# Threshold attention and a squared-ReLU layer on one core: the order of the first loads, of attention's last two periods, of the second layer's weight loads, and of some sums of x

## The chip, the cores and the metric

The kernel runs on one core of a Trainium2 chip. The metric is the device time of one execution in microseconds (us). TensorE (PE in the profile) does the matrix products, VectorE (DVE), ScalarE (ACT) and GpSimd (POOL) the elementwise work, and SyncE (SP) issues nearly all transfers, in program order.

## The reference

Attention first, on 8 batches, 8 heads, 576 positions and 64 columns, then a layer on 4608 tokens, all in float32 (the two weight matrices come as float64 and are converted in the kernel):

```python
scores = scale * np.matmul(q, k.transpose(0, 1, 3, 2))
thresh = np.max(scores, axis=-1, keepdims=True) - tau
scores = np.where(scores >= thresh, scores, -1000000000.0)
scores = scores - np.max(scores, axis=-1, keepdims=True)
attn = np.exp(scores)
attn = attn / (np.sum(attn, axis=-1, keepdims=True) + 1e-09)
x = np.matmul(attn, v)      # then (B,H,S,D) -> (B*S, H*D) = 4608 x 512
h = np.maximum(x @ w_in, 0.0)        # w_in 512 x 2048
out = h * h @ w_out                  # w_out 2048 x 512
```

## The kernel before, in words

**Attention.** Heads are taken two at a time: 32 pairs, loaded with `load_q`, `load_k` and `load_v`. A pair has four full tiles of 128 queries, and two pairs share a fifth made of their rests, so there are 144 units (`NU`). A period p works on units 2p and 2p + 1 at different stages at once. `period(p)` holds its steps by name, and a list of names gives their order: `CONVERTING` while weight chunks are being converted, `PLAIN` afterwards, and `BEGIN_WITH[p]` for a period with an order of its own (0 and 1 before the change). A trailing "-" means the step of the period before, "--" of two before; `step` first runs any earlier period's step of that name that was not run yet, and each (step, period) runs once.

The steps that matter here: SA, SB and RA, RB are the scores (L458); top is the reduction on VectorE (L476); pow and mask are exp on ScalarE (L486) and masking on VectorE (L491). The masked weights of two units m are turned on TensorE in three fills (`fill`, L402): V covers the first eight of 18 half tiles (chunks 0 to 3), W the two of chunk 4, U the eight of chunks 5 to 8. V and U go to the one buffer pair `pt`, W to two middle banks of the scores' memory `sc`. Q adds the scales (L541). eV, eW and eU copy a fill out to the arena (`filled`, L549, on ScalarE), PV is the product with the values (`values`, L558, 72 matmuls over nine chunks), x copies the result out of banks 0 and 5 of `sc` (L689 on ScalarE, L691 on VectorE), xm scales the rest (L701 on GpSimd) and queues the store to `xT` in DRAM. The program declares by hand which instructions on `sc` do not depend on each other: `touch` records each with its banks and key, and pairs of kinds listed in `MEET` keep their dependency.

**SyncE's order.** The loads of queries and keys are queued in `wanted` and issued a few at a time by the steps "ahead" and "more" (`ahead(5)`); "fetch" issues the load of a weight chunk (L194) two periods ahead; the main loop issues `load_v(p)` after periods 0, 1 and 2 (L337). A pair's keys come with L320 and L327, the queries' rest with L328, into the same tile `rn` as the rest keys. Every transfer waits for the transfer eight places ahead of it in that order to be done, so at most eight are out at once.

**The layers.** Both products are done with seven instead of eight block products, nested twice, so a pass has 7 x 7 = 49 products. `hidden_layer` runs nine passes (`PASSES`): one for the first 512 tokens, six in pairs that share weights, two single ones. After each product a tick runs `also`, in which work for later passes is placed by block i (0 to 6, in the order `OUTER`) and place `at` in it (0 to 6). In `inner` the copy of the first product (L794, ScalarE) and the additions to products (L125, VectorE) free TensorE's six banks; GpSimd adds the finished blocks (L125). `square` squares a finished block (L951, L952) and stores it to `g` in DRAM (L955, or L958 for paired passes), at least six ticks after it is done.

`before_x` makes sums of x for the next pair of passes during passes 0, 2, 4 and 6. A sum (`sum_v`) is a ScalarE copy of one operand to the small buffer `c` (L838) and, a tick later, the operation on VectorE (L122 or L125). The two sums `turned_` read a part of x that is loaded (L820) at block 2, place 1, and are placed at block 3, places 0 and 3.

`output_layer` runs nine times, on the operands g (`load_g`, L1064) and the second layer's weights. These 49 weight tiles stand in DRAM (`w`) and overwrite the first layer's in `wall` once those are done with: `reload(at)` (L1207). Tile `at` is first used at product `at` of the first output pass, that is tick 49 + `at` counted from the start of the last hidden pass. Before the change one reload follows each tick from tick 10 on: 39 in the last hidden pass, ten in the first output pass. In the first output pass `load_g(1, ...)` loads eight tiles at block 2, place 0 (tick 63), and eight at block 2, place 6 (tick 69); the first sums of the second eight are at block 4.

Of the kernel before, what the change touches and what calls it, by code (L numbers as in the profile page):

```python
# [48 lines left out]
def kernel(  # L49
# [322 lines left out]
    behind = mybir.DependencyInfo(mybir.DependencyClass.Sync, mybir.DependencyReason.DATA)  # L372

    Q_RING, K_RING, W_RING = 3, 4, 2
    MEET = (("scores", "turnedq", (Q_RING,)), ("scores", "turnedk", (K_RING,)), ("last scores", "turnedk", (K_RING,)), ("values", "weights", (W_RING,)), ("x", "weights", (W_RING,)))

    def touch(what, made, at, size, key=0):

# [162 lines left out]
                    made = nc.tensor.matmul(to, wide, ident[rows, rows], start=True, stop=True)  # L541
                    touch("turns", made, at + r * BANK, BANK)

    def filled(m, f, pt, at=None):

        first, count = FILLS[f]
        count += 2 * (f == "W")
        to = wT[m][:, ds(weight_at(first) * P, count * P)]
        touch("weights", nc.scalar.copy(joined(to), whole(pt, 0, count)), at, 2 * BANK, m)  # L549

    def values(m):

        for c in range(CH):
            for u in range(2):
                for s, (i, _, count, row) in enumerate(halves(2 * m + u)):
                    for j in range(2):
                        rows = ds(j * D, D)
                        made = nc.tensor.matmul(  # L558
                            sc[ds(u * D, D), ds(5 * j * BANK + row, count)], loaded_v[i][rows, (c - (u != j)) % CH, :],
                            wT[m][rows, ds(weight_at(2 * c + u) * P + row, count)],  # L560
                            start=(c == 0 and s == 0), stop=(c == CH - 1), skip_group_check=True,
                        )
                        touch("values", made, 5 * j * BANK, BANK, m)

    def valued(m):

# [71 lines left out]
        """.split(),  # L638
    }

    def spots():
        return [(sc[:, ds(b * BANK + REST, (FULL + 1) * HALF)], b * BANK) for b in (1, 4)]

    def middle():
        return sc[:, 2 * BANK : 4 * BANK].rearrange("p (r n) -> p r n", r=2)

    def period(p):

# [2 lines left out]
        late, pt = {"W": []}, {}  # L651

        def fills(f, m):
            if has(2 * m):
                pt[f] = pt_pool.tile([P, 2, BANK], FP32, tag="pt", name="pt")
                fill(m, f, pt[f])

        def evict(f, m):
            if has(2 * m):
                filled(m, f, pt[f], 2 * BANK if f == "W" else None)  # L660

        def W():
            if has(2 * m + 2):
                pt["W"] = middle()
                fill(m + 1, "W", pt["W"], 2 * BANK)

        def Q():
            if has(2 * m + 2):
                spread_sums(m + 1, pt["W"], 2 * BANK)

        def turn_some():
            free = None
# [42 lines left out]
        def every(key):  # L715
# [10 lines left out]
            "c1": lambda: convert1(begun(p)), "c2": lambda: convert2(begun(p)),  # L726
            "c3": lambda: convert3(begun(p)), "c4": lambda: convert4(begun(p - 1)),
            "c5": lambda: convert5(begun(p - 1)), "c6": lambda: convert6(begun(p - 1)),
            "s1": lambda: sums_due(p) and sums_step(), "s2": lambda: sums_due(p) and p < 60 and sums_step(), "ahead": lambda: ahead(5), "more": lambda: ahead(5),
            "fetch": lambda: (fetch(begun(p + 2)), fetch(begun(p + 3)) if p > 1 else None), "put": put, "give": lambda: ask(False),  # L730
        }
        steps["over"] = lambda: do(a, "over")
# [170 lines left out]
    def before_x(steps, i, at):  # L903

        if (i, at) in BEFORE_X:
            ask_x(steps, *BEFORE_X[i, at])
        turned_ = lambda: outer_x(steps, minus, 6, 2, None)
        added = lambda: outer_x(steps, plus, 6, 6, 1)
        fourth = lambda: outer_x(steps, minus, 4, 2, 6)
        if i == 4 and at < len(steps):  # L910
            nc.scalar.copy(slot_x(steps[at], 7), slot_x(steps[at], 6))
        work = {
            (3, 0): lambda: turned_()[0:1], (3, 3): lambda: turned_()[1:],
            (4, 2): lambda: added()[0:1], (4, 5): lambda: added()[1:],
            (5, 1): lambda: fourth()[0:1], (5, 4): lambda: fourth()[1:],
            (5, 6): lambda: inner_x(steps, 1),
        }
        return work.get((i, at), list)()
# [242 lines left out]
    with tc.manual_schedule():  # L1161
        with ExitStack() as stack:
# [24 lines left out]
            turn(0, 1, spots(), nc.vector.tensor_copy)()  # L1187
            for p in range(FIRST_PERIOD, NU // 2 + 6):
                run_period(p)
                if 0 <= p < 3:  # L1190
                    load_v(p)
                if X_FIRST <= p < X_FIRST + 4:
                    load_x(0, XPARTS[p - X_FIRST :][:1])
                if p == X_FIRST + 4:
                    summing.append(prepare_x(0, lambda op, out, x, y: op(nc.gpsimd, out, x, y)))
# [6 lines left out]
        def reload(at):  # L1202

            m, k = OUTER[at // 7], INNER[at % 7]
            t = weight_tile(W_OUT, m, k)
            at = 8 * made_at(m) + made_at(k)
            nc.sync.dma_start(out=t[:, :], in_=w_dram[ds(at * P, P), :])  # L1207

        chain_at, over_at = 26 * BANK, 26 * BANK + 2 * BANK
        halves_ = [(m, k, h) for m, k in blocks_out[EARLY:] for h in range(2)]  # L1210
# [69 lines left out]
        for n, (steps, h) in enumerate(PASSES):  # L1280
# [14 lines left out]
            def also(m, at):  # L1295
# [91 lines left out]
```

## Time and profile before

| | us |
|---|---|
| median of 3 runs | 1282.17 (1278.94 to 1284.23) |
| profiled execution | 1281.21 |
| its span, first to last instruction | 1279.1 |
| TensorE busy in the span | 1252.5 |
| attention ends (first product of the hidden layer) | 495.87 |
| first output pass goes on after its first four products | 889.50 |

A timeline row reads: start, duration, engine, line, operation, written <- read, shape, count, and in brackets the idle time of the engine just ahead of it with what ended it. A row of windows reads: the stretch, its length, the busy time of PE, PEld, DVE, ACT and POOL with the number of instructions, the clock granted to TensorE (1.00 is full), the busy share of the transfer engines, and GB/s.

### The profile page before, as it was taken

What the parts mean: (1) busy time and instruction counts of PE and PEld (TensorE: products, weight loads), DVE (VectorE), ACT (ScalarE), POOL (GpSimd) and SP (SyncE); (2) the same over time, 40 slices, a digit from 0 to 9 for tenths busy, and PEclk for the clock granted to TensorE, in tenths of its full rate; (3) what the DMA queues carried; (4) which work ended last, traced back from release to release, by engine and by line L of the source; (5) the groups of instructions that cost most, each with busy time, mean ns of one, the idle gap of its engine ahead of it and who ended that gap; (6) DMA issues with size and microseconds to landing.
All of it is one profiled execution on the core that took longest, in us unless ns stands there. A gap on an engine that the chain in (4) does not pass through costs nothing.

```text
span 1279.1 us, 55422 instructions
## 1 busy us (share of the span) xinstructions
PE 1252.5 (98%) x22991; PEld 1093.8 (86%) x22991; DVE 987.5 (77%) x2384; ACT 845.6 (66%) x1537; POOL 982.4 (77%) x1070
## 2 busy tenths in 40 slices
PE   7999999999999999999999999999999999999998
PEld 5777777777777778988888888999999999999998
DVE  6999999999999995886887877876646654665563
ACT  6999999999999994665765857665424432433240
POOL 2899898877776542987897989858777877787776
PEclk9999999999999999999999999999999999999999
DMA  7566667434333323658767868589654235523511
GB/s 185 131 170 149 176 191 195 117 93 104 85 86 86 80 58 84 203 170 232 209 190 215 229 169 239 164 304 361 240 164 162 65 109 167 167 57 112 167 35 35
DMA packets 291450, 196.81 MB, mean 154 GB/s; under 512 B 100096, under 2 KB 252160, under 8 KB 291200
## 3 DMA queue, kind: packets, MB, share of 16 engines
q1 hardware_dynamic: 289888, 192.87, 52.6%
q8 instruction: 181, 2.97, 1.0%
q14 instruction: 69, 0.57, 0.2%
q10 hardware_dynamic: 1312, 0.41, 0.1%
HBM read 120.85 MB, written 72.35 MB: 151 GB/s over the span
## 4 chain that ended last, share of the span: by engine, by line
PE 74%; DMA 2%; DVE 2%; ACT 1%; issue 1%; SPq 0%; POOL 0%; DVEq 0%; POOLq 0%; ACTq 0%
PE po L799 27%; PE ph L982 18%; PE ph L799 10%; PE sc L558 7%; PE sc L458 6%; PE pt L402 4%; PE sc L541 1%; PE sc L422 1%; DVE arena L125 1%; DMA arena<-g 1%; ACT c L838 1%; PE sc L402 0%; DMA wall<-w 0%; DVE arena L122 0%; ACT arena L951 0%
## 5 line engine op out<-in xcount | busy, mean ns | idle before, releaser
L125 POOL TENSOR_TENSOR arena<-arena 128x512 f32<-128x512 f32 (+1 forms) x314 | 378.3, 1224 | 130.5 <-DVE arena L125 118.7
L799 PE MATMUL po<-wall,arena 128*64 128x128 f32 x7056 | 388.3, 273 | 4.2 <-ACT arena L794 2.8
L799 PEld LDWEIGHTS po<-wall,arena 128*64 128x64 f32 x7056 | 386.7, 137 | 5.6 <-ACT arena L794 3.8
L125 DVE TENSOR_TENSOR arena<-ph,arena 128x512 f32<-128x512 f32 x378 | 254.8, 689 | 79.9 <-PE ph L982 31.9
L122 POOL TENSOR_TENSOR arena<-arena 128x128 f32<-128x128 f32 (+1 forms) x322 | 265.6, 826 | 23.8 <-DMA arena<-w 8.2
L982 PE MATMUL ph<-arena,wall 128*128 128x256 f32 x1176 | 256.6, 380 | 1.6 <-DVE arena L125 1.3
L982 PEld LDWEIGHTS ph<-arena,wall 128*128 128x128 f32 x1176 | 222.1, 190 | 36.0 <-DVE arena L125 5.8
L125 DVE TENSOR_TENSOR arena<-po,arena 128x128 f32<-128x128 f32 x378 | 108.0, 289 | 160.6 <-PE po L799 156.8
L491 DVE SCALAR_TENSOR_TENSOR arena<-arena 128x576 f32<-128x576 f32 x288 | 226.0, 821 | 0.0
L486 ACT ACTIVATE arena<-arena 128x576 f32<-128x576 f32 x288 | 213.3, 778 | 13.2 <-DVE arena L476 13.1
L476 DVE TENSOR_SCALAR_CACHE_REDUCE arena<-sc 128x576 f32<-128x576 f32 x288 | 203.3, 753 | 18.8 <-issue 7.7
L838 ACT COPY c<-arena 128x512 f32<-128x512 f32 (+1 forms) x295 | 169.0, 578 | 72.9 <-DVE arena L122 35.5
L458 PE MATMUL sc<-arena 64*64 64x512 f32 (+1 forms) x2304 | 178.8, 415 | 5.6 <-ACT arena L549 1.0
L558 PE MATMUL sc<-arena 64*64 64x128 f32 (+1 forms) x5760 | 165.9, 261 | 1.3 <-ACT arena L549 0.8
L122 DVE TENSOR_TENSOR arena<-arena,c 128x512 f32<-128x512 f32 x235 | 154.4, 666 | 12.7 <-ACT c L838 8.3
L558 PEld LDWEIGHTS sc<-arena 64*64 64x64 f32 x5760 | 150.7, 133 | 4.9 <-issue 1.0
L549 ACT COPY arena<-pt 128x1024 f32<-128x1024 f32 x144 | 145.7, 1012 | 3.8 <-PE pt L402 3.2
L458 PEld LDWEIGHTS sc<-arena 64*64 64x64 f32 x2304 | 76.7, 134 | 70.8 <-issue 46.5
L794 ACT COPY arena<-po 128x128 f32<-128x128 f32 x63 | 16.6, 263 | 181.8 <-PE po L799 177.0
L799 PE MATMUL ph<-arena,wall 128*64 128x128 f32 x2352 | 129.2, 273 | 0.6 <-DVE arena L691 0.6
L799 PEld LDWEIGHTS ph<-arena,wall 128*64 128x64 f32 x2352 | 128.3, 137 | 1.4 <-issue 1.0
L483 POOL TENSOR_SCALAR arena<-arena,tau_p 128x2 f32<-128x2 f32 x144 | 83.7, 581 | 57.9 <-DVE arena L476 43.5
(54 smaller groups left out, 1139.6 us busy)
## 6 DMA issues: line engine op xcount, KB each, us to landing
arena<-g SPq DMA_DIRECT2D x144, 256.0 KB, 5.1
g<-arena SPq DMA_DIRECT2D x192, 128.0 KB, 2.9
w<-arena SPq DMA_DIRECT2D x60, 256.0 KB, 3.0
wall<-w SPq DMA_DIRECT2D x49, 256.0 KB, 5.5
g<-arena SPq DMA_DIRECT2D x48, 256.0 KB, 3.7
arena<-w SPq DMA_DIRECT2D x44, 256.0 KB, 3.4
arena<-in_v_dram SPq DMA_DIRECT2D x32, 288.0 KB, 3.8
out_dram<-arena SPq DMA_DIRECT2D x70, 128.0 KB, 2.9
```

The source lines that it names most:

```text
L122: e.tensor_tensor(out=out, in0=x, in1=y, op=ALU.subtract)
L125: e.tensor_tensor(out=out, in0=x, in1=y, op=ALU.add)
L458: made = nc.tensor.matmul(sc[at, ds(to, count)], lhs, kT[rows, ds(at_k, count)], start=True, stop=True)
L476: made = nc.vector.tensor_scalar(out=s[:, j, :], in0=sc[:, ds(at, S)], scalar1=1.0, scalar2=None, op0=ALU.mult, op1=ALU.min, accum_out=nmx ...
L483: nc.gpsimd.tensor_scalar(out=thr, in0=nmx, scalar1=tau_p[:, :], scalar2=None, op0=ALU.add)
L486: nc.scalar.activation(out=w[:, :, j, :], in_=of(j), func=AF.Exp, bias=nmx[:, j : j + 1], scale=-1.0)
L491: nc.vector.scalar_tensor_tensor(out=w[:, :, j, :], in0=of(j), scalar=thr[:, j : j + 1], in1=w[:, :, j, :], op0=ALU.is_le, op1=ALU.mult, a ...
L549: touch("weights", nc.scalar.copy(joined(to), whole(pt, 0, count)), at, 2 * BANK, m)
L558: made = nc.tensor.matmul(sc[ds(u * D, D), ds(5 * j * BANK + row, count)], loaded_v[i][rows, (c - (u != j)) % CH, :], wT[m][rows, ds(weigh ...
L799: nc.tensor.matmul(to[cols], lhs[:, cols], rhs, start=start, stop=stop, skip_group_check=True)
L838: nc.scalar.copy(c, y)
L982: nc.tensor.matmul(to[:, 2 * j : 2 * j + 2, :], W_IN[m, k][:, ts(2 * h + j, P)], part_x(steps, k, m), start=(not more and j == 0), stop=Tr ...
```

## The change

- `load_v` is issued after periods 0, 2 and 3 instead of 0, 1 and 2, and "more" issues seven loads of keys instead of five. In SyncE's order the second pair's rest keys (L327) and queries' rest (L328) now stand ahead of one value load and two weight chunks, and the third pair's keys ahead of two value loads and a chunk.
- Period 73 has an order of its own that runs the steps of the last units to the end: the values of unit 70 come ahead of V of unit 71, and U of unit 71 goes to banks 3 and 4 of `sc` (W to 1 and 2) and is copied out by VectorE. The values of every unit are recorded in three kinds, by chunk, of which only chunk 4 meets W's copy and only the later ones U's.
- Reloads skip every sixth tick: 33 in the last hidden pass, 16 in the first output pass, the last at tick 67, so that four stand between the two groups of `load_g(1, ...)`.
- The two sums `turned_` move from places 0 and 3 of block 3 to 2 and 4.

```diff
-    MEET = (("scores", "turnedq", (Q_RING,)), ("scores", "turnedk", (K_RING,)), ("last scores", "turnedk", (K_RING,)), ("values", "weights", (W_RING,)), ("x", "weights", (W_RING,)))
+    MEET = (("scores", "turnedq", (Q_RING,)), ("scores", "turnedk", (K_RING,)), ("last scores", "turnedk", (K_RING,)), ("values", "weights", (W_RING,)), ("last values", "last weights", (W_RING,)), ("x", "weights", (W_RING,)))
...
-    def filled(m, f, pt, at=None):
+    def filled(m, f, pt, at=None, last=False):
...
-        touch("weights", nc.scalar.copy(joined(to), whole(pt, 0, count)), at, 2 * BANK, m)
+        copy_by = nc.vector.tensor_copy if last else nc.scalar.copy
+        kind = "last weights" if last else "weights"
+        touch(kind, copy_by(joined(to), whole(pt, 0, count)), at, 2 * BANK, m)
...
-                        touch("values", made, 5 * j * BANK, BANK, m)
+                        part = "first values" if c < FULL else "values" if c == FULL else "last values"
+                        touch(part, made, 5 * j * BANK, BANK, m)
...
+    BEGIN_WITH[NU // 2 + 1] = """
+        give eU-- powA0-- V-- powA1-- eV-- maskA1-- PV-- powB1-- powB0-- maskA0-- U- W-- Q-- x--
+        maskB1-- maskB0-- eW-- over- inv- eU- xm-- PV- x- V- eV- W- Q- eW- xm- U eU PV x xm
+        """.split()
...
+    LAST = NU // 2 - 1
+    def w_bank(m):
+        return 1 if m == LAST else 2
+    def two_banks(first):
+        return sc[:, ds(first * BANK, 2 * BANK)].rearrange("p (r n) -> p r n", r=2)
...
         def fills(f, m):
-            if has(2 * m):
+            if (f, m) == ("U", LAST):
+                pt[f] = two_banks(3)
+                fill(m, f, pt[f], 3 * BANK)
+            elif has(2 * m):
...
         def evict(f, m):
-            if has(2 * m):
-                filled(m, f, pt[f], 2 * BANK if f == "W" else None)
+            if (f, m) == ("U", LAST):
+                filled(m, f, pt[f], 3 * BANK, True)
+            elif has(2 * m):
+                filled(m, f, pt[f], w_bank(m) * BANK if f == "W" else None)
...
-            "s1": lambda: sums_due(p) and sums_step(), "s2": lambda: sums_due(p) and p < 60 and sums_step(), "ahead": lambda: ahead(5), "more": lambda: ahead(5),
+            "s1": lambda: sums_due(p) and sums_step(), "s2": lambda: sums_due(p) and p < 60 and sums_step(), "ahead": lambda: ahead(5), "more": lambda: ahead(7),
...
-            (3, 0): lambda: turned_()[0:1], (3, 3): lambda: turned_()[1:],
+            (3, 2): lambda: turned_()[0:1], (3, 4): lambda: turned_()[1:],
...
-                if 0 <= p < 3:
-                    load_v(p)
+                if p in (0, 2, 3):
+                    load_v(max(p - 1, 0))
...
+        reloads = iter(range(49))
+        def reload_due(tick):
+            if tick > 9 and tick % 6 != 3:
+                at = next(reloads, None)
+                if at is not None:
+                    reload(at)
...
-                if 7 * i + at > 9:
-                    reload(7 * i + at - 10)
+                reload_due(7 * i + at)
...
-                if n == 0 and 7 * i + at < 10:
-                    reload(39 + 7 * i + at)
+                if n == 0:
+                    reload_due(49 + 7 * i + at)
```

More of the change, by code (lines that the diff above doesn't have):

```diff
@@ L639 @@
     }
+    BEGIN_WITH[NU // 2 + 1] = """
+        give eU-- powA0-- V-- powA1-- eV-- maskA1-- PV-- powB1-- powB0-- maskA0-- U- W-- Q-- x--
+        maskB1-- maskB0-- eW-- over- inv- eU- xm-- PV- x- V- eV- W- Q- eW- xm- U eU PV x xm
+        """.split()
     def spots():
         return [(sc[:, ds(b * BANK + REST, (FULL + 1) * HALF)], b * BANK) for b in (1, 4)]
-    def middle():
-        return sc[:, 2 * BANK : 4 * BANK].rearrange("p (r n) -> p r n", r=2)
+    LAST = NU // 2 - 1
[3 more added lines that the diff above has]
+        return sc[:, ds(first * BANK, 2 * BANK)].rearrange("p (r n) -> p r n", r=2)
     def period(p):
@@ L658, in evict @@
         def evict(f, m):
-            if has(2 * m):
-                filled(m, f, pt[f], 2 * BANK if f == "W" else None)
+            if (f, m) == ("U", LAST):
+                filled(m, f, pt[f], 3 * BANK, True)
+            elif has(2 * m):
+                filled(m, f, pt[f], w_bank(m) * BANK if f == "W" else None)
         def W():
             if has(2 * m + 2):
-                pt["W"] = middle()
-                fill(m + 1, "W", pt["W"], 2 * BANK)
+                pt["W"] = two_banks(w_bank(m + 1))
+                fill(m + 1, "W", pt["W"], w_bank(m + 1) * BANK)
         def Q():
             if has(2 * m + 2):
-                spread_sums(m + 1, pt["W"], 2 * BANK)
+                spread_sums(m + 1, pt["W"], w_bank(m + 1) * BANK)
         def turn_some():
```

## The prediction

> **What bounds the kernel now.** I read the page's head and its groups first, then TensorE's timeline for each of its pauses, then the engine or queue that each pause names.
>
> ```profile
> span 1279.1 us, 55422 instructions
> PE 1252.5 (98%) x22991; PEld 1093.8 (86%) x22991; DVE 987.5 (77%) x2384; ACT 845.6 (66%) x1537; POOL 982.4 (77%) x1070
> ...
> L476 DVE TENSOR_SCALAR_CACHE_REDUCE arena<-sc 128x576 f32<-128x576 f32 x288 | 203.3, 753 | 18.8 <-issue 7.7
> ```
>
> TensorE works for 1252.5 of 1279.1 us. The change takes away no matmul, so it can win only from the 26.6 us of pauses and from stretches at a lower granted clock. Its four parts touch four places, each with a pause of its own. The order on TensorE, VectorE and ScalarE is the same in both kernels up to the last two periods, so nothing is paid 72 times.
>
> **1. Keys' loads first (start).**
>
> ```profile
> 28.15 0.34 PE L422 MATMUL sc<-ident,arena 64*128 64x64 f32 x2 [1.62 <-DMA arena<-in_q_dram]
> ```
> ```profile
> 19.20 0.61 SPq L337 DMA_DIRECT2D arena<-in_v_dram  x1
> 19.85 1.38 SPq L194 DMA_DIRECT2D wall<-in_moe_w_in_dram  x2
> 21.27 0.49 SPq L327 DMA_DIRECT2D arena<-in_k_dram  x1
> 21.81 0.60 SPq L328 DMA_DIRECT2D arena<-in_q_dram  x1
> ```
> ```profile
> 26.47:29.88 3.41, 1.79 (x28) 0.98 (x26) 0.74 (x5) 1.90 (x3) 0.90 (x2) 1.00 0.81 247
> 29.88:33.30 3.42, 3.42 (x46) 1.98 (x48) 2.78 (x8) 2.28 (x4) 1.96 (x2) 0.50 0.28 62
> ```
> ```profile
> 29.74 0.76 DVE L476 TENSOR_SCALAR_CACHE_REDUCE arena<-sc 128x576 f32<-128x576 f32 x1 [2.67 <-issue]
> ...
> 33.69 0.76 DVE L476 TENSOR_SCALAR_CACHE_REDUCE arena<-sc 128x576 f32<-128x576 f32 x1 [1.03 <-ACT arena L208]
> ```
>
> The windows' columns are stretch, length, busy us of PE, PEld, DVE, ACT, POOL, granted clock, DMA share, GB/s. TensorE stands from 26.53 to 28.15 for the queries' rest of the second pair (L328), issued at 21.81: 6.3 us from issue to use. In SP's order one value load and two weight chunks stand ahead of it; the change puts all three behind it and sends the rest keys (L327) and L328 at about 19.20 and 19.85. Even at 6.3 us it is there at 26.2, before 26.53. What moves back has room: the values of pair 1 are read two periods later, the chunks are converted a period later.
>
> In the stretch with the pause TensorE was busy 1.79 of 3.41 us, and the next, equally long, ran at 0.50. Without the pause I expect no halved stretch: 1.62 + 3.42 x 0.5 = 3.3. VectorE is late next: it stood 2.67 + 1.03 = 3.7 us here, and after 33.69 has hardly a gap, so at most 3.7 passes through. Two reductions (0.75 each) must free banks before the next scores; I take 0.3 off: **-3.0**. Ends: 0 (something else in that tile is as late) and -3.7.
>
> [...]
>
> **2. Attention's last two periods.**
>
> ```profile
> 488.23 0.71 PE L402 MATMUL pt<-ident,arena 64*128 64x64 f32 x16 [1.68 <-ACT arena L549]
> 488.87 2.20 PE L558 MATMUL sc<-arena 64*64 64x128 f32 x72
> 491.00 0.71 PE L402 MATMUL pt<-ident,arena 64*128 64x64 f32 x16
> 491.54 0.29 PE L402 MATMUL sc<-ident,arena 64*128 64x64 f32 x4
> 491.76 0.46 PE L541 MATMUL sc<-ident,arena 64*64 64x64 f32 x16
> 492.97 2.33 PE L558 MATMUL sc<-arena 64*64 64x128 f32 x108 [0.75 <-ACT arena L549]
> 495.87 0.40 PE L799 MATMUL ph<-arena,wall 128*64 128x128 f32 x3 [0.57 <-DVE arena L691]
> ```
>
> Pauses 1.68 + 0.75 + 0.57 = 3.0. The first waits for the eviction (L549) that frees the one pt pair; the change puts value matmuls of unit 70 there. Their first four of nine chunks read only V, already evicted: 2.2 x 4/9 = 1.0 of matmuls at once, from about 486.5; the fifth needs eW, the others U's eviction, which ends just as the pause did, at 488.2. So 1.0 of 1.68 is filled, and a fifth chunk of 0.24, less a wait of 0.05: 1.15 gained. The second pause goes as well: U of unit 71 has banks of its own and is turned (0.7) while ScalarE evicts V and W, so values follow with no wait: 0.75. New is a VectorE copy of 1024 columns that U's half of the last values waits for. No row has it; 576 columns from the same memory take 0.753 (L476), so 0.75 to 1.5 (twice that), by columns 1.3. The first five chunks, 2.3 x 5/9 = 1.3, cover it; at 1.5 it costs 0.2. Behind the copy VectorE has only the last product with the scales (L691), which waits for the values anyway. The last 0.57 stays. Of 1.15 + 0.75 I take 0.1 off for waits in between: **-1.8**; ends 0 and -2.4.
>
> **3. Sums of x later.**
>
> ```profile
> 605.06 85.91 PE L982 MATMUL ph<-arena,wall 128*128 128x256 f32 x392 [0.74 <-DVE arena L125]
> 691.56 105.53 PE L982 MATMUL ph<-arena,wall 128*128 128x256 f32 x484 [0.59 <-DVE arena L125]
> ```
> ```profile
> 603.09 1.29 ACT L838 COPY c<-arena 128x512 f32<-128x512 f32 x2 [1.61 <-DMA arena<-xT]
> ```
> ```profile
> 603.71 0.69 DVE L122 TENSOR_TENSOR arena<-arena,c 128x512 f32<-128x512 f32 x1 [1.21 <-ACT c L838]
> ```
>
> ScalarE's copy waits for x, VectorE's sum stands behind the copy, and behind the sum stand the additions that free TensorE's banks. No ScalarE work is queued between old and new place, so the copy still waits for x; but the sum now stands behind two more additions, two products later, each four records of 85.91 / 392 us, so 0.88; and 1.76 exceeds 1.21. Both pauses go: **-1.3**; ends 0 and -1.3. Each sum, 0.69, fits the two other passes, which have no pause at this place.
>
> **4. Second layer's weights at an even pace.**
>
> ```profile
> 889.50 35.21 PE L799 MATMUL po<-wall,arena 128*64 128x128 f32 x592 [2.81 <-ACT arena L794]
> ```
> ```profile
> 889.18 0.27 ACT L794 COPY arena<-po 128x128 f32<-128x128 f32 x1 [4.81 <-POOL arena L125]
> ...
> 917.99 1.26 ACT L838 COPY c<-arena 128x512 f32<-128x512 f32 x2 [3.61 <-DMA arena<-g]
> ```
> ```profile
> 874.23 8.73 POOL L125 TENSOR_TENSOR arena<-arena 128x512 f32<-128x512 f32 x7
> 883.43 1.28 POOL L125 TENSOR_TENSOR arena<-arena 128x512 f32<-128x512 f32 x1 [0.47 <-DMA g<-arena]
> 886.67 3.71 POOL L125 TENSOR_TENSOR arena<-arena 128x512 f32<-128x512 f32 x3 [1.96 <-DVE arena L125]
> ```
> ```profile
> 884.64 0.69 DVE L125 TENSOR_TENSOR arena<-ph,arena 128x512 f32<-128x512 f32 x1 [2.99 <-DMA g<-arena]
> ```
> ```profile
> 868.09 9.50 SPq L1207 DMA_DIRECT2D wall<-w  x14
> 877.94 0.32 SPq L955 DMA_DIRECT2D g<-arena  x1
> ...
> 903.94 10.29 SPq L1064 DMA_DIRECT2D arena<-g  x16
> ```
> ```profile
> 886.62:890.03 3.41, 0.60 (x12) 0.54 (x12) 0.96 (x3) 0.76 (x2) 3.36 (x3) 1.00 1.01 362
> 890.03:893.45 3.42, 3.42 (x38) 3.42 (x34) 2.43 (x6) 2.39 (x6) 2.90 (x3) 0.50 1.06 395
> ```
>
> VectorE stands 2.99 for a store of g whose place it overwrites; that store stands in SP's queue behind weight loads of 9.50 / 14 = 0.68 each. GpSimd, ScalarE's copy and TensorE follow. In the new order four or five fewer weights are ahead of these stores: 2.7 to 3.4 us, about the whole 2.99. GpSimd is late next: free at 882.96, it has two more additions after the one at 883.43, so the copy can come at 882.96 + 3 x 1.25 = 886.7 instead of 889.18: 2.4, and the halved stretch after it, 1.7, goes too: 4.1.
>
> Not all is kept. ScalarE later waits until 917.99 for the thirteenth of sixteen g tiles. It was issued at 903.94 + 12 x 0.64 = 911.7 and used 6.3 later. Now four weights stand between the eighth tile and the ninth: 2.6. The first tile's load is behind stores of squares that ScalarE makes, at most 3.5 earlier. So the thirteenth lands 0.9 earlier, with a little for a queue less full 1.2, and VectorE, whose sums wait for ScalarE's copies and whose additions free TensorE's banks, sets TensorE's time from there. I take **-1.2**. Ends: -4.1, and +4.3 if the loads start no earlier (2.6, and a halved stretch, 1.7).
>
> ```profile
> DMA to landing us min/median/max: 3.0/6.0/6.9
> ```
>
> That is the landing of the sixteen g tiles (L1064) from 900 to 920; the slower rival uses its 6.9.
>
> **Sum.** -3.0 - 1.8 - 1.3 - 1.2 = -7.3 on the profiled execution's 1281.21: 1273.9. The median of the runs, 1282.17, is 1.0 above it, so 1274.9. Measurement tells about 0.5%, 6.4 us, from no change: 1275.8 is the border.
>
> **Rivals.**
> - *Nothing handed back*: g's tiles land in time. 7.3 + 2.9 = 10.2: 1272.0. For it: the stores of squares ahead of the loads come earlier too. Against: TensorE arrives 4.1 earlier at a queue with four more loads. 0.12.
> - *The halved clock stays* at the start, by a cause other than the pause; only 1.6 of 3.0 is won: 1276.3. [...] Against it: both halved stretches quoted follow a stretch half idle or more. 0.10.
> - *The start isn't relieved*: the wait names the last to land, and the rest keys may be as late. 4.3: 1277.9. 0.10.
> - *It doesn't do what it says* in x or the tail: the copy is late again, or VectorE's copy of U is dearer than its cover. About 1.5 less: 1276.4. 0.08.
> - *Slower*: the four weights ahead of g's second eight tiles. At most eight loads are out at once in SP's order; if the loads begin at 903.94 as before and each round of eight takes the longest, 6.9, the needed tile, now seventeenth, lands with the third round at 924.6, 6.6 late, and a halved stretch adds 1.7. With 6.1 won elsewhere: +2.2, 1284.4. It decides from a landing at 922.4; before that it only eats the gain. 0.06 for that, 0.06 for a milder one, about 1280.
>
> **Chances.** Forecast 0.48, own range 1272.9 to 1276.7. Faster by over 0.5%: 0.7 of that, the first rival, and the near edges of two others: 0.52. Within: 0.43. Slower by over 0.5%: only the tail of the last, 0.05. The range 1271.0 to 1279.8 leaves out the slower one and the outer ends.
>
> **What would show it.** Right: no TensorE wait for q's load near 26.5 and a clock of 1.00 from 29.88; the last values followed by L817's first product some 1.8 us sooner after the same point; no pause at 605 and 691; no 2.99 wait on a store of g, no halved clock near 891, and ScalarE's wait for g longer than 3.6. Wrong: a wait for L327, a pause moved to another tile's turn, or the 917.99 landing at 919 or later once the earlier gains are taken off.

## The result, and the profile after

| | before | changed kernel |
|---|---|---|
| median, us (lowest to highest) | 1282.26 (1276.88 to 1290.20), 20 executions | 1278.46 (1275.55 to 1282.14), 20 executions |
| ratio, 95% interval | | 0.9969 [0.9955, 0.9983] |
| profiled execution, its span | 1281.21, 1279.1 | 1279.41, 1277.4 |

The change wins 3.8 us, 0.31%: in the direction and inside the range that were given, half of the 7.3 that were forecast, and within the 0.5% called "no change" above. In the profile's head of the changed kernel TensorE's work is the same, and what is left of the span beside it has shrunk from 26.6 to 24.8:

```profile
span 1277.4 us, 55414 instructions
...
PE 1252.6 (98%) x22991; PEld 1092.4 (86%) x22991; DVE 989.6 (77%) x2385; ACT 844.7 (66%) x1536; POOL 981.7 (77%) x1070
```

**Start.** The same two windows as before, in the changed kernel; no wait of TensorE for queries is left there, and the half clock behind it is gone:

```profile
26.47:29.88 3.41, 3.41 (x84) 2.44 (x78) 3.32 (x9) 3.41 (x8) 1.93 (x3) 1.00 0.78 210
29.88:33.30 3.42, 3.33 (x98) 2.51 (x93) 3.42 (x11) 3.41 (x7) 2.72 (x3) 1.00 0.53 158
```

**Attention's last two periods**, TensorE's timeline after: of the pauses of 1.68 and 0.75 only 0.47 is left, inside the value products of unit 70; unit 71's (490.33) start without a pause, and the 0.57 before the hidden layer stays.

```profile
487.42 1.10 PE L560 MATMUL sc<-arena 64*64 64x128 f32 x32 [0.47 <-ACT arena L551]
488.45 0.71 PE L402 MATMUL pt<-ident,arena 64*128 64x64 f32 x16
...
490.33 2.48 PE L560 MATMUL sc<-arena 64*64 64x128 f32 x108
493.37 4.88 PE L817 MATMUL ph<-arena,wall 128*64 128x128 f32 x85 [0.57 <-DVE arena L709]
```

**Sums of x.** The pauses at 605 and 691 are gone. Three others come up a block later, which the kernel before didn't have. First TensorE after, then ScalarE and GpSimd after:

```profile
614.37 5.78 PE L1000 MATMUL ph<-arena,wall 128*128 128x256 f32 x24 [0.35 <-DVE arena L125]
620.58 1.13 PE L1000 MATMUL ph<-arena,wall 128*128 128x256 f32 x4 [0.42 <-ACT arena L812]
622.18 8.12 PE L1000 MATMUL ph<-arena,wall 128*128 128x256 f32 x33 [0.47 <-DVE arena L125]
```
```profile
602.34 1.31 ACT L856 COPY c<-arena 128x512 f32<-128x512 f32 x2 [3.35 <-DMA arena<-xT]
...
614.16 0.63 ACT L969 ACTIVATE arena<-arena 128x512 f32<-128x512 f32 x1 [2.47 <-POOL arena L125]
```
```profile
599.83 0.45 POOL L122 TENSOR_TENSOR arena<-arena 128x128 f32<-128x128 f32 x1 [2.40 <-DMA arena<-w]
607.74 0.99 POOL L122 TENSOR_TENSOR arena<-arena 128x128 f32<-128x128 f32 x2 [2.40 <-DMA arena<-w]
```

GpSimd stands twice for 2.40 for a load of `w`. These are the chains of weight sums (`chain_out`): a load of a quarter of four weight tiles (L1298), four subtractions on GpSimd (L122) six ticks later, a store (L1303). ScalarE's activation and the additions queued behind GpSimd are late with it.

The three new pauses are 1.24 together, about as much as the two that went (1.33), and yet the section below grows by 1.2. The rest is not in marked pauses: between ScalarE's 17th and 62nd copy (counted as below) TensorE's busy time is 276.44 after and 275.40 before, at a clock of 1.00 in both. Product by product, TensorE falls behind the kernel `chain` below by 2.5 from 614 to 624, and by 0.8 more at the same blocks of the next two passes.

**Second layer.** TensorE and ScalarE after. The stall at 889.50 has shrunk from 2.81 to 0.77. ScalarE's wait for g's thirteenth tile has grown from 3.61 to 5.77, and TensorE now stands 1.76 at 920.67:

```profile
886.20 12.67 PE L817 MATMUL po<-wall,arena 128*64 128x128 f32 x224 [0.77 <-ACT arena L812]
899.84 17.69 PE L817 MATMUL po<-wall,arena 128*64 128x128 f32 x320 [0.98 <-ACT arena L812]
...
920.67 2.27 PE L817 MATMUL po<-wall,arena 128*64 128x128 f32 x32 [1.76 <-ACT arena L812]
```
```profile
885.88 0.27 ACT L812 COPY arena<-po 128x128 f32<-128x128 f32 x1 [2.77 <-POOL arena L125]
...
916.24 1.27 ACT L856 COPY c<-arena 128x512 f32<-128x512 f32 x2 [5.77 <-DMA arena<-g]
```

SyncE's queue after shows why: eight g tiles, then four weights, then eight g tiles.

```profile
900.03 3.90 SPq L1082 DMA_DIRECT2D arena<-g  x8
904.08 2.65 SPq L1225 DMA_DIRECT2D wall<-w  x4
907.09 6.11 SPq L1082 DMA_DIRECT2D arena<-g  x8
```

**Where the time went, section by section.** TensorE's order of instructions is the same in both kernels but for the last two periods, and so is that of ScalarE's copies of its results, so the start of the same instruction can be compared. Here are the sections between six such points in the timelines, one profiled execution for each kernel: the first product of unit 1's values (L558 before, L560 after), that of unit 69's, and ScalarE's copies of TensorE's results (L794, L812) counted from the hidden layer on: the 1st, 17th, 62nd and 71st (in the profile before these lie at 33.40, 483.04, 497.04, 594.85, 871.89 and 934.06; 1st to 17th is 97.8 in every one, and from the 71st to the end 345.1). The kernels other than the first two are those of the experiments.

| kernel | start to unit 1 | unit 1 to 69 | last two periods | copies 17 to 62 | copies 62 to 71 |
|---|---|---|---|---|---|
| before | 33.40 | 449.64 | 14.00 | 277.04 | 62.17 |
| changed | 31.26 | 450.97 | 12.32 | 278.26 | 61.68 |
| start_only | 29.95 | 454.34 | 15.61 | 280.33 | 61.65 |
| tail_only | 33.77 | 449.91 | 12.32 | 281.46 | 61.58 |
| x_only | 34.00 | 449.97 | 15.67 | 277.90 | 58.66 |
| reload_only | 35.92 | 450.31 | 15.59 | 278.20 | 61.21 |
| again | 31.01 | 452.28 | 12.32 | 278.19 | 61.03 |
| hold | 29.91 | 449.38 | 12.32 | 278.12 | 58.50 |
| noreload | 31.16 | 449.86 | 12.32 | 278.92 | 60.97 |
| chain | 30.95 | 447.62 | 12.32 | 274.75 | 61.72 |
| both | 31.26 | 449.98 | 12.32 | 274.94 | 58.48 |
| chain_noreload | 30.09 | 453.07 | 12.32 | 274.78 | 59.15 |
| nox | 30.58 | 449.94 | 12.32 | 278.98 | 61.38 |
| chain_nox | 31.45 | 449.98 | 12.32 | 277.25 | 61.30 |

Between the first two rows: -2.1, +1.3, -1.7, +1.2, -0.5, in all -1.8, against forecast -3.0, 0, -1.8, -1.3, -1.2. The two profiled executions differ by less than the medians do (1.8 against 3.8). Single executions of one program differ by some us (the 20 of the kernel before run from 1276.88 to 1290.20), so sizes are read from the table at a place, and sums from the medians.

### The profile page after: what moved, and what is told of

Same layout as the page of the kernel before. It is cut to its first block, busy times and chain, and to the rows that moved or that the text cites. A ratio compares the mean times of both kernels' runs of the same rounds, so it can differ in the third digit from the quotient of the medians.

```text
span 1277.4 us, 55414 instructions
## 1 busy us (share of the span) xinstructions
PE 1252.6 (98%) x22991; PEld 1092.4 (86%) x22991; DVE 989.6 (77%) x2385; ACT 844.7 (66%) x1536; POOL 981.7 (77%) x1070
## 4 chain that ended last, share of the span: by engine, by line
PE 71%; DMA 3%; ACT 2%; DVE 2%; issue 1%; POOL 1%; SPq 0%; DVEq 0%; ACTq 0%; POOLq 0%
PE po L817 27%; PE ph L1000 15%; PE ph L817 10%; PE sc L560 7%; PE sc L458 6%; PE pt L402 4%; PE sc L541 1%; DVE arena L125 1%; PE sc L422 1%; DMA w<-arena 1%; ACT arena L969 1%; ACT c L856 1%; DMA arena<-g 1%; POOL arena L125 1%; DMA wall<-w 1%
## 5 line engine op out<-in xcount | busy, mean ns | idle before, releaser
L122 POOL TENSOR_TENSOR arena<-arena 128x128 f32<-128x128 f32 (+1 forms) x322 | 265.4, 826 | 33.2 <-DMA arena<-w 17.3
L1000 PE MATMUL ph<-arena,wall 128*128 128x256 f32 x1176 | 257.7, 380 | 1.8 <-DVE arena L125 0.8
L1000 PEld LDWEIGHTS ph<-arena,wall 128*128 128x128 f32 x1176 | 221.9, 190 | 37.3 <-DVE arena L125 6.7
L560 PE MATMUL sc<-arena 64*64 64x128 f32 (+1 forms) x5760 | 165.6, 261 | 0.6 <-ACT arena L551 0.5
L122 DVE TENSOR_TENSOR arena<-arena,c 128x512 f32<-128x512 f32 x235 | 154.4, 666 | 12.6 <-ACT c L856 9.3
L560 PEld LDWEIGHTS sc<-arena 64*64 64x64 f32 x5760 | 150.5, 133 | 4.0 <-ACT arena L551 0.7
L812 ACT COPY arena<-po 128x128 f32<-128x128 f32 x63 | 16.6, 263 | 179.8 <-PE po L817 177.0
```

Source lines behind the costliest of these rows:

```text
L122: e.tensor_tensor(out=out, in0=x, in1=y, op=ALU.subtract)
L560: made = nc.tensor.matmul(sc[ds(u * D, D), ds(5 * j * BANK + row, count)], loaded_v[i][rows, (c - (u != j)) % CH, :], wT[m][rows, ds(weigh ...
L1000: nc.tensor.matmul(to[:, 2 * j : 2 * j + 2, :], W_IN[m, k][:, ts(2 * h + j, P)], part_x(steps, k, m), start=(not more and j == 0), stop=Tr ...
```

## The experiments

### One part at a time

Each is the kernel before with one part of the change: "more" with seven keys and `load_v` after periods 0, 2 and 3; period 73's own order with its banks and copies; the places of the two sums; the pace of the reloads.

```diff
-            ... "more": lambda: ahead(5),
+            ... "more": lambda: ahead(7),
...
-                if 0 <= p < 3:
-                    load_v(p)
+                if p in (0, 2, 3):
+                    load_v(max(p - 1, 0))
```
```diff
-    MEET = (... ("values", "weights", (W_RING,)), ("x", "weights", (W_RING,)))
+    MEET = (... ("values", "weights", (W_RING,)), ("last values", "last weights", (W_RING,)), ("x", "weights", (W_RING,)))
...
+    BEGIN_WITH[NU // 2 + 1] = """
...
```
```diff
-            (3, 0): lambda: turned_()[0:1], (3, 3): lambda: turned_()[1:],
+            (3, 2): lambda: turned_()[0:1], (3, 4): lambda: turned_()[1:],
```
```diff
-                if 7 * i + at > 9:
-                    reload(7 * i + at - 10)
+                reload_due(7 * i + at)
...
```

> Only the order of the first loads is changed. Theory A (each part keeps what its place shows): TensorE's wait of 1.6 us for the queries' rest near 26.5 us goes, the second value product starts about 2.1 us earlier, the fifth one about 2.3, and that shift stays to the end: about -2.3 us of time. Theory B (transfers that don't move with TensorE take it back): the same shift at 40 us, but under 0.5 us of it left at the end of attention.

> Only attention's last two periods are changed. Theory A: from the third-last value product to the hidden layer's first product 1.7 us less than before (11.14 instead of 12.83), kept to the end: about -1.7 us. Theory B: the same 1.7 at that place, but the waits for transfers in the hidden layer and at the first output pass take it back: under 0.5 us at the end.

> Only the two sums of x are later. Theory A (my forecast): the pauses at 605 and 691 us (0.74 and 0.59) go, -1.3 us at the end of the hidden layer. Theory B (read from the trace after): the pauses go, but GpSimd's chain of weight sums, which waits for loads from DRAM with GpSimd's later additions queued behind it, then holds TensorE instead: of 1.9 us won by the two places 1.2 or more is lost one or two blocks later, net between -0.7 and 0.

> Only the pace of the second layer's weights is changed. Theory A (my forecast): the pause of 2.8 us after the first four output products shrinks to under 1, the clock stays full after it, and ScalarE's wait for the g tiles hands back all but about 1.2 us. Theory B (read from the trace after): the same, but the g tiles land only about 0.5 us earlier, so -0.5 us at the end. Theory C: the whole 4 us is kept, if the wait for g doesn't grow.

A ratio with its interval is not exactly the quotient of the two medians, here and below.

| kernel | median (range), 12 executions | ratio to before (1282.57) |
|---|---|---|
| start_only | 1281.43 (1275.86 to 1286.96) | 0.9991 [0.9973, 1.0010] |
| tail_only | 1279.54 (1274.01 to 1283.98) | 0.9983 [0.9964, 1.0002] |
| x_only | 1281.78 (1276.15 to 1287.26) | 0.9994 [0.9976, 1.0012] |
| reload_only | 1284.71 (1280.80 to 1288.26) | 1.0009 [0.9991, 1.0028] |

By time none of the four can be told from no change; reload_only's median lies 2.1 above the one before, where each of its theories had it below. By place two can. Every profile with the start part reaches unit 1 in 29.91 to 31.45, every one without it in 33.40 to 35.92; the means are 30.8 (of 10) and 34.3 (of 4), 3.5 apart. Every profile with the tail part takes 12.32 for the last two periods, the four without it 14.00 to 15.67. The other two show nothing clear at their places: with the x part and the old chains the hidden layer takes 277.90 to 278.92 (mean of five 278.28), without it 277.04 to 281.46 (mean of five 279.20, chain_nox left out); with the reload part the last column has 61.03 to 61.72 (hold and both left out), without it 58.66 to 62.17. In start_only's profile the 3.45 won at unit 1 is gone by unit 69, 484.29 against 483.04, as its second theory has it.

In start_only the pause that x's sums make is not 0.74 but 2.35, and a half clock follows (TensorE's row, then the window behind it):

```profile
609.53 8.77 PE L982 MATMUL ph<-arena,wall 128*128 128x256 f32 x32 [2.35 <-DVE arena L125]
```
```profile
609.80:613.20 3.40, 3.40 (x10) 2.69 (x11) 2.38 (x4) 0.00 (x0) 1.35 (x2) 0.56 0.74 200
```

So the pause that the x part removes costs from 0.7 us (0.71 in reload_only) to 4.8 (3.06 in tail_only, and half of the 3.41 behind it), by execution; the profile before shows the cheap form. And in x_only the second layer's stall is short although its weights come at the old pace:

```profile
890.92 12.67 PE L799 MATMUL po<-wall,arena 128*64 128x128 f32 x224 [0.77 <-ACT arena L794]
```

### Taking away what gives back

Four kernels, beside each other: the changed kernel again; with the last reloads held until g's sixteen tiles are issued; without the reload part; with the chains of weight sums set apart.

```diff
-            if tick > 9 and tick % 6 != 3:
+            if tick > 9 and tick % 6 != 3 and not 62 < tick < 70:
```
```diff
-                reload_due(7 * i + at)
+                if 7 * i + at > 9:
+                    reload(7 * i + at - 10)
...
-                    reload_due(49 + 7 * i + at)
+                if n == 0 and 7 * i + at < 10:
+                    reload(39 + 7 * i + at)
```
```diff
-        CHAINS = [49 * n + c for n in range(NSTEP - 1) for c in (-4, 6, 12, 18, 24, 36)[n == 0:]][0 : len(chains)]
+        CHAINS = [49 * n + c for n in range(NSTEP - 1) for c in (-4, 6, 13, 21, 29, 37)[n == 0:]][0 : len(chains)]
```

> The changed kernel once more, beside the three below. Theory A (its parts work at their places, in every execution): no wait of TensorE for queries near 26.5 and a clock of 1.00 after it; no pause before the first value product of the hidden layer's start beyond 0.6; a wait of GpSimd for the weight chain's loads near 600 and 608 of 2 us or more; ScalarE's wait for g's thirteenth tile 5 to 6 us. Time 1277 to 1280. Theory B (what was seen in one execution was that execution's luck): at least one of these is missing, or the waits for queries inside attention add up to over 4 us in this one.

> The changed kernel, but no second-layer weight is loaded in ticks 64 to 68, so that the last five loads go behind g's second eight tiles instead of between the eighth and the ninth. Theory A (the weights between g's tiles give back what the reload part wins): the ninth to sixteenth tile are issued up to 2.6 us earlier, ScalarE's wait for the thirteenth falls from 5.8 to about 3, and the kernel is 2 to 3 us faster than the changed one: 1275.5 to 1276.5. Theory B (the landing is set by the tiles' own time in the queue and what is out with them, not by the four weights): the wait stays above 5, and the time within 1 us of the changed kernel's.

> The changed kernel without its reload part: the second layer's weights are loaded one a tick, as before the change. Theory A (the reload part takes away a stall of 2.8 and its half clock, and gives as much back at g's thirteenth tile): within 1 us of the changed kernel, 1277.5 to 1279.5, with the stall near 885 there again and a wait for g of about 3.5. Theory B (moving x already takes that stall away, as the kernel with x alone seemed to show): no stall of TensorE near 885, ScalarE's wait for g below 4, and 2 to 3 us faster than the changed kernel: 1275 to 1276.5.

> The changed kernel, with the six chains of weight sums in a period of 49 ticks begun at ticks -4, 6, 13, 21, 29, 37 instead of -4, 6, 12, 18, 24, 36, so that two chains that share a buffer stand 15 ticks or more apart and not 12: the load of one no longer waits in SyncE's queue for the store of the one before the last. Theory A (the sums of x gained 1.9 us at their two places, and GpSimd's wait for those loads gave it back at the next blocks): GpSimd's waits for loads of w near 600 to 612 fall from 5.2 to under 2, TensorE's pauses near 614 to 622 go, and the kernel is about 2 us faster than the changed one: 1276 to 1277. Theory B (what comes back there is set by x's or g's transfers, or by VectorE): pauses of the same sum stay near 610 to 625, and the time is within 1 us of the changed kernel's. Theory C: sums fall on ticks where GpSimd is full, pauses come up elsewhere, and it is slower by 1 us or more.

| kernel | median (range), executions | ratio to before (1281.03) |
|---|---|---|
| again | 1278.55 (1275.55 to 1281.12), 12 | 0.9980 [0.9965, 0.9995] |
| hold | 1274.11 (1271.63 to 1277.39), 10 | 0.9954 [0.9937, 0.9970] |
| noreload | 1275.53 (1272.35 to 1280.01), 12 | 0.9961 [0.9944, 0.9979] |
| chain | 1273.29 (1272.02 to 1274.36), 6 | 0.9942 [0.9922, 0.9963] |

**again** shows the same at all four places, the chain's waits (5.3 in all) and the wait for g (5.1) among them, as its first theory has it. Its waits for queries inside attention came to 1.7.

**hold.** SyncE's queue, ScalarE and TensorE in it: the sixteen tiles go out in one piece, the wait for the thirteenth is 2.65 instead of 5.77, and TensorE's pause of 1.76 is gone.

```profile
896.94 9.53 SPq L1082 DMA_DIRECT2D arena<-g  x16
906.75 2.87 SPq L1225 DMA_DIRECT2D wall<-w  x4
```
```profile
910.03 1.95 ACT L856 COPY c<-arena 128x512 f32<-128x512 f32 x3 [2.65 <-DMA arena<-g]
```
```profile
896.75 25.79 PE L817 MATMUL po<-wall,arena 128*64 128x128 f32 x464 [0.98 <-ACT arena L812]
```

The last column falls from 61.0 and 61.7 to 58.5. The four weights between the tiles (the expectation says five) gave back 2.5 to 3.2, as its first theory has it. The median fell by 4.4 against again, more than that theory's 2 to 3; 1.9 or so of it isn't found at this place.

**chain.** Waits of the changed kernel from 590 to 622, GpSimd's and then SyncE's, and the same two of chain. The columns are the sum in us, how often, and the longest:

```profile
POOL arena L122 <- DMA arena<-w: 5.2, 3, 2.4
```
```profile
SPq L1298 <- DMA w<-arena: 4.0, 2, 2.6
```
```profile
POOL arena L122 <- DMA arena<-w: 1.6, 2, 0.9
```
```profile
SPq L1298 <- DMA w<-arena: 2.3, 2, 1.9
```

Chains that share a buffer begin 12 ticks apart, twice in a pass, in the changed kernel. The load of the later one stands in SyncE's queue until the store of the earlier has landed, and GpSimd stands for the load. At 15 ticks and more both waits shrink, and from the hidden layer to 930 TensorE has no wait for GpSimd's or VectorE's sums in the hidden passes (L1000) any more:

```profile
PE po L817 <- ACT arena L812: 3.6, 3, 1.8
PE po L817 <- DVE arena L125: 0.3, 1, 0.3
```

Its hidden layer takes 274.75 against 278.2 in the two profiles of the changed kernel, 3.5 less. The new ticks also move the subtractions themselves to other ticks, which no run separates from the shorter waits. The median is 5.3 below again's, beyond its theory's 2, and as with hold more than the place shows. In the profiles the rest lies ahead of the hidden layer, where the three kernels do the same: unit 69 starts at 478.57 in chain and 479.29 in hold, but at 482.23 and 483.29 in the two profiles of the changed kernel. Whether that belongs to the kernels or to these executions is open.

**noreload** has the trace of its first theory, a wait for g of 3.65 among it, and the time of its second. Its stall in the second layer is 2.24, without a half clock, and its last column, 60.97, is again's, so by the trace the reload part is worth nothing net. Its median is 3.0 lower, though.

```profile
887.11 12.68 PE L817 MATMUL po<-wall,arena 128*64 128x128 f32 x224 [2.24 <-ACT arena L812]
```

### Both mends, and each part without the other

All but nox have the new ticks of chain. both adds the line of hold, chain_noreload the lines of noreload; nox and chain_nox put the two sums back:

```diff
-            (3, 2): lambda: turned_()[0:1], (3, 4): lambda: turned_()[1:],
+            (3, 0): lambda: turned_()[0:1], (3, 3): lambda: turned_()[1:],
```

> The changed kernel with both mends: chains begun at ticks -4, 6, 13, 21, 29, 37, and no second-layer weight loaded in ticks 64 to 68. Theory A (two separate hand-backs, each at its own place): no pause at the blocks after 605, ScalarE's wait for g's thirteenth tile about 3, and both gains add: 2 to 3 us faster than with the new chains alone, 1270 to 1272. Theory B (whatever is won earlier is taken by g's tiles at the end): within 1 us of the new chains alone, 1272.5 to 1274.5, with a wait for g of 5 or more.

> Chains begun at the new ticks, and the reload part undone (one second-layer weight a tick from tick 10 on). Theory A (by the traces the reload part takes away about 2.9 near 885 and gives back about as much near 918): within 1 us of the kernel with the new chains and the reload part, 1272.3 to 1274.3. Theory B (the reload part costs more than it brings, as the medians with and without it have it, 1278.6 and 1275.5): 2 to 3 us faster than with it, 1270 to 1271.5, with a stall near 880 below 1.5.

> The changed kernel without its x part: the first two sums of x back at their old places. Theory A (the x part takes two pauses away and GpSimd's wait for the chain gives 2.5 back, so it is worth between -1 and +3 by execution): pauses before the blocks at 605 and 691 again, of 0.7 each or of 2.4 and more with a half clock behind, no pauses at 614 to 622, and a time between 1277.5 and 1281. Theory B (the x part costs more than it brings): 1275.5 to 1277.

> Chains begun at the new ticks, and the x part undone. Theory A (the chains' loads and the sums of x are two separate causes): the pauses before the blocks at 605 and 691 are back, and it is 2 to 5 us slower than the new chains with the x part, 1275 to 1278. Theory B (ScalarE's copy waits for x because SyncE's queue is held by a chain's load that waits for a store; with the chains apart x lands in time wherever its sums stand): within 1 us of the new chains with the x part, 1272.3 to 1274.3, and no pause at 605.

| kernel | median (range), executions | ratio to before (1281.38) |
|---|---|---|
| both | 1271.78 (1270.87 to 1274.48), 6 | 0.9925 [0.9897, 0.9954] |
| chain_noreload | 1273.97 (1271.91 to 1276.41), 10 | 0.9941 [0.9921, 0.9962] |
| nox | 1278.99 (1277.57 to 1283.94), 12 | 0.9986 [0.9967, 1.0006] |
| chain_nox | 1278.27 (1276.19 to 1280.03), 12 | 0.9969 [0.9953, 0.9986] |

**both** is the fastest kernel of the study, 0.75% below the one before. Its waits of TensorE from 490 to 925:

```profile
PE po L817 <- ACT arena L812: 1.8, 2, 1.0
PE po L817 <- DVE arena L125: 0.6, 1, 0.6
PE ph L817 <- DVE arena L709: 0.6, 1, 0.6
```

The two hand-backs are separate, as its first theory has it: the hidden layer takes 274.94 (chain 274.75), the last column hold's 58.5. It is 1.5 below chain by median and 3.2 by the last column.

**nox and chain_nox**, with the kernels that have the x part, make a square of medians:

| | sums of x at their old places | moved |
|---|---|---|
| chains 12 ticks apart | 1278.99 (nox) | 1278.46, 1278.55 (changed, again) |
| chains 15 ticks apart | 1278.27 (chain_nox) | 1273.29 (chain) |

Either alone is worth 0.5 to 0.7 us by the medians, both together 5.7. At its place, the hidden layer's section, it is 278.98 (nox), 278.2 (changed, again), 277.25 (chain_nox) and 274.75 (chain): there the moved sums alone win 0.8, the new ticks alone 1.7, and both 4.2. In nox the pause is there, 2.53 at 602.64; in chain_nox as well, 1.13 and 0.42, though GpSimd has no wait for the chain there. That speaks against chain_nox's second theory, in which x would land in time once SyncE's queue is freer; its time lies 0.3 beyond the first theory's 1275 to 1278. The pause goes because the sum stands behind two more additions, and most of what that wins is kept only if the chains don't take it. TensorE's rows of nox and of chain_nox:

```profile
602.64 27.61 PE L1000 MATMUL ph<-arena,wall 128*128 128x256 f32 x123 [2.53 <-DVE arena L125]
```
```profile
602.15 28.02 PE L1000 MATMUL ph<-arena,wall 128*128 128x256 f32 x126 [1.13 <-DVE arena L125]
...
688.09 12.14 PE L1000 MATMUL ph<-arena,wall 128*128 128x256 f32 x55 [0.42 <-DVE arena L125]
```

**chain_noreload** is 0.7 above chain, within the 1 us of its first theory, but its stall is 0.78, as the second had it. So the medians disagree about the sign of the reload part: here it wins 0.7, while noreload (3.0 below again) and reload_only (2.1 above before) have it cost 2 to 3.

The profiles show what the parts do to each other. Without the reload part the stall is 2.81, 2.48 and 2.48, each with a half clock, in the three kernels with x's sums at their old places (before, start_only, tail_only), and 0.77, 2.24 and 0.78, without one, in the three with them moved (x_only, noreload, chain_noreload). So with x moved the stall is gone in two profiles of three, and the half clock in all three, without the reload part; why is open. ScalarE's wait for g is 2.8 to 3.7 without the reload part and 5.1 to 5.8 with it (hold and both left out). Beside the moved sums the last column is then 58.66, 60.97 and 59.15 without the reload part, and 61.68, 61.03 and 61.72 with it: there it costs about 1.9 at its place. With the four weights behind g's tiles (both) it is 58.48: 2.2 below chain_noreload by median, but only 0.7 at the place.

## Why the prediction was right and where it was wrong

1. **Start, -3.0: right in mechanism and size.** -2.1 in the pair, -3.5 between the means. In all ten profiles with the part TensorE's wait for the queries near 26.5 is gone and the clock from 26.47 to 33.30 is 1.00; in the four without it the wait is 1.62 to 3.65 and the window behind it has 0.50 to 0.62. That refutes the rival with a half clock of another cause. Not foreseen: the section from unit 1 to 69, where nothing is changed, took 449.6 to 450.3 in the four profiles without the part and 447.6 to 454.3 in the ten with it, 0.8 longer on average. Waits for queries come up at other places, up to 1.9 in all (without the part up to 1.2), the longest in start_only, with a half clock behind it:

```profile
158.69 0.41 PE L422 MATMUL sc<-ident,arena 64*128 64x64 f32 x2 [1.94 <-DMA arena<-in_q_dram]
```

   Whether the part causes them or they differ by execution is open.

2. **Last two periods, -1.8: right.** -1.7 in the pair. VectorE's copy of U cost TensorE at most 0.15: its last 108 value products ran without a pause, in 2.48 against 2.33. Where the pause of 1.68 brings a half clock, as in three of the four profiles without the part, the part is worth up to 3.35.

3. **Sums of x, -1.3: the step that failed.** "Both pauses go" held; that the 1.3 is then won did not. It asked what is late next on VectorE and found nothing; it didn't ask GpSimd. The profile before already shows GpSimd's wait for the chain's load, here from 590 to 622; it ends with a load that stands behind a store, whenever TensorE comes:

```profile
POOL arena L122 <- DMA arena<-w: 3.2, 3, 1.6
```

   TensorE came earlier, and this wait grew from 3.2 to 5.2. At this one place it varies by execution (4.8 in nox, without the x part), but over the hidden layer (17th to 62nd copy) GpSimd's waits for loads of w sum to 8.2 to 10.2 in the five profiles with old chains and the sums at their old places, 11.0 to 14.4 in the five with them moved, and 0.4 to 3.5 in the four with the new ticks. In the pair the hidden layer got 1.2 longer instead of 1.3 shorter, a miss of 2.5, outside the ends "0 and -1.3". chain shows the cause: with most of the wait gone, the hidden layer is 2.3 shorter than before.

   The pair is an unlucky one, though: its kernel before shows the cheapest of the five forms of the pauses. By the means of five profiles each (279.20 and 278.28) the x part wins 0.9, near the 1.3 but not by its sum: the pauses cost more than the 1.33 read from one profile, and the hand-back, put at nothing, took most of what that adds.

4. **Reloads, -1.2: right about both waits, too large by 0.7 in the pair.** The stall fell to 0.77, there is no half clock behind it, and ScalarE's wait for g's thirteenth tile grew past 3.6, to 5.77. The landing came 1.75 earlier (916.24 against 917.99), but TensorE arrived there with 1.27 already won, so 0.5 is the part's own. The price that the step named, four weights between the tiles, is shown by hold: 2.5 to 3.2. The loads of g began 3.9 earlier (900.03), where the step had at most 3.5. What it did not see is that x's part by itself takes the same stall away in two profiles of three, so that beside it the reload part wins nothing at its place and costs about 1.9 there in the mean of three profiles each. The rival with nothing handed back was put at 1272.0; the kernel that takes both hand-backs away has 1271.8, by a change that the prediction hadn't thought of for x.

5. **The sum.** The terms that were added are gains at places. Of the 7.3, x's 2.5 and the reloads' 0.7 were taken back at the next wait behind them; that leaves 4.1, beside 3.8 measured by the medians. That these two agree is partly luck: the pair's own places come to -1.8, since the start gave 0.9 less than its term and attention's unchanged part took 1.3, and no table here places the 3.8. The chance for faster by over 0.5% was put at 0.52, and the time fell within 0.5%; the chance for the latter was 0.43. Too much weight was put on terms without asking, for each, what is late next on every engine.

## What to carry to other kernels

A pause taken away is a gain only up to the next wait whose end doesn't depend on the engine that got faster: look on every engine behind the pause, GpSimd and the transfer queue too, for a wait that is already there and can grow. Here GpSimd's for the chain's load grew from 3.2 to 5.2, ScalarE's for g from 3.61 to 5.77. Two buffers used in turn with a load, a sum and a store each need room for the store to land before the next load (SyncE waits 4.0 for it in the changed kernel, 2.3 in chain); three ticks more were worth 3.5 us at their place here, with x's sums moved, and 5.3 by the medians. Two parts that remove the same stall don't add (it is 0.77 in x_only, and 0.77 with all four parts). A change whose parts win 1 to 3 us each is judged at its places in several executions, which differ by as much.

## What the runs showed of the hardware

The same pause doesn't always bring a half clock. TensorE stands 1.68 in the last two periods in all four kernels without the tail part. At full clock it costs 1.68, with the half clock 1.6 more (14.00 against 15.6). nox's pause of 2.53 was followed by a clock of 1.00, start_only's of 2.35 by a half clock.

In start_only the half clock behind the pause of 1.68 is a stretch of 3.41 us, 489.91 to 493.32. The second pair of rows is the stretch ahead of it and this one. The first pair is the kernel before, in stretches of that length counted on from its half clock at 29.88:

```profile
487.28:490.70 3.42, 2.47 (x84) 2.40 (x88) 0.63 (x3) 1.91 (x2) 0.69 (x2) 1.00 0.33 65
490.70:494.11 3.41, 2.66 (x110) 2.28 (x104) 0.29 (x1) 1.77 (x3) 0.46 (x1) 1.00 0.19 38
```
```profile
486.50:489.91 3.41, 1.73 (x55) 1.45 (x50) 2.66 (x10) 2.60 (x5) 1.79 (x4) 1.00 0.21 41
489.91:493.32 3.41, 3.41 (x70) 3.29 (x70) 0.00 (x0) 1.01 (x1) 0.00 (x1) 0.50 0.22 43
```

In start_only the whole pause lies in one stretch, in which TensorE is busy 1.73 of 3.41; before, it is split over two, with 2.68 (483.87 to 487.28) and 2.47.

No rule follows from this. In the kernel before the half clocks at 29.88 and 890.03 come behind stretches with 1.79 and 0.60 busy, but the one at 19.64 behind 1.91. In the changed kernel one at 16.90 comes behind 1.67, and another at 20.32 behind 2.36, while stretches with as little, 1.94 at 218.29 and 1.66 at 918.02, are followed by a clock of 1.00. The kernels were made for other ends; no run moved a pause against these stretches, and what decides is not shown.
